# A decode step with cached attention, written anew on named semaphores: TensorE loops over the pairs, all queries come first, V stays a pair behind K

## The chip, the cores and the metric

The kernel runs on one core of a Trainium2 chip. The metric is the time of one execution on the device in microseconds; a kernel's time is the median of its runs. The engines are called as in the profile: PE (TensorE), DVE (VectorE), ACT (ScalarE), POOL (GpSimd) and SP (SyncE, which here issues DMAs); "SPq" is an issue by SP, "PEld" a weight load of PE.

## What is computed

One decode step for two tokens (one per batch entry), all in float32. `x` is normalised, attends with 32 heads to a cache of 8192 keys and values per head, and the result is gated by a small MLP:

```python
xn = layernorm(x)                                  # x: 2 x 1 x 512
q  = (xn @ wq), cut into 32 heads of 128           # wq: 512 x 4096
p  = softmax(q . k_cache * 128**-0.5)              # k_cache: 2 x 32 x 8192 x 128
s  = (p @ v_cache), heads side by side, @ wo       # wo: 4096 x 512
y  = layernorm(xn)
g  = silu(gelu(y @ w1 + b1) @ w2 + b2)             # w1: 512 x 1376, w2: 1376 x 512
out = x + s * g
```

K and V are 268 MB each; every byte is used once.

## The kernel before

The 64 (batch, head) rows are handled as 32 pairs, `n` = 0 to 31, of two heads each. A pair's K is one tile of 128 partitions x 128 rows x 128 columns, 8.39 MB: partitions 0 to 63 hold the first head, 64 to 127 the second, each partition 128 keys. A V tile looks the same. Three such tiles fill nearly all of the on-chip memory: two buffers for K (`kpool`) and one for V (`vpool`). At the start the second K buffer holds `wq` and the V buffer holds the start-up data: `w1`, `w2`, `x`, the normalised `x`, the projected queries, `sel`, `z` and `th` (`take`, L80 to 95).

The setup loads `w1`, `w2` and K0 (in two halves) from SP and the small inputs and `wq` from ACT. It normalises `x`, computes the MLP and its gate (`mlp`, L190 to 225; DVE writes `gate` at L224 and L225), projects the queries (`project_q`, L237), gathers them (`gather_q`, L247) and spreads the first pair's query over 128 partitions (`queries`, L258). Then SP issues K1 and V0 (L271, L272).

The loop over the pairs (L355 to 400) is written out by hand; each engine runs its instructions in the order of the program, and waits are put in by the framework from what reads and writes what. For pair `n`:

- DVE multiplies K by the query in two halves (L280) and sums over the columns in two halves (L285), which gives 128 scores per partition. The maximum over the free axis (L289) is transposed by PE (L293); DVE reduces it to one negative maximum per head (`nm`, L298) one half of a product *later*, in pair `n+1`.
- PE spreads `nm` over the partitions (L306), ACT copies it (L308) and takes the exponentials into `PZ` (L313). A matmul adds the row sums to `OA` (L319).
- PE multiplies V by the exponentials (`weighted`, L328: 32 calls, each two matmul instructions in the trace), ACT copies the result (L335), PE adds up the columns (L338), DVE spreads them (L343) and PE places them in `OA` (L351). The weighted sum for pair `n-1` stands in pair `n`.
- SP issues V of pair `n` when the weighted sum of `n-1` has released the one V buffer (L372), and K of `n+2` when DVE has summed pair `n` (L396).

Towards the end this order changes (`LATE`, L354): the weighted sums of the last pairs come a pair later, V30 goes into a K buffer, V31 is loaded in five pieces, and `wo` into the other K buffer in six (`WO_PIECES`, with the last two rows cut by partitions at 120, L404 to 407). At the end DVE divides `OA` by the row sums (L419, L421), PE multiplies by `wo` (`acc`, L424), DVE applies the gate and adds `x` (L428, L429), and SP and ACT store the two rows.

Of the kernel before, what the change touches and what calls it, by code (L numbers as in the profile page):

```python
# [1 line left out]

# [16 lines left out]
@with_exitstack  # L19
def decode_kernel(ctx: ExitStack, tc: tile.TileContext, x, kc, vc, wq, wo, w1, b1, w2, b2, out):  # L20
    nc = tc.nc
# [21 lines left out]
    ZP = P - U * PH  # L43

    consts = ctx.enter_context(tc.tile_pool(name="consts", bufs=1))
    kpool = ctx.enter_context(tc.tile_pool(name="kpool", bufs=2))
    vpool = ctx.enter_context(tc.tile_pool(name="vpool", bufs=1))
    small = ctx.enter_context(tc.tile_pool(name="small", bufs=2))
    ps_c = ctx.enter_context(tc.tile_pool(name="ps_c", bufs=1, space=bass.MemoryType.PSUM))
    ps_s = ctx.enter_context(tc.tile_pool(name="ps_s", bufs=4, space=bass.MemoryType.PSUM))  # L50
    ctx.enter_context(tc.manual_schedule())


    K, V = {}, {}
# [3 lines left out]
    def load(dst, src, cuts):  # L58
        for a, e in zip(cuts, cuts[1:]):
            nc.sync.dma_start(dst[:, a:e], src[:, a:e])  # L60

    def load_k(n, cuts=(0, KP)):
        K[n] = kpool.tile([P, KP, DH], F32, tag="k", name=f"k{n}")
        load(K[n], kf[n], cuts)

    def load_v(n, cuts=(0, KP), pool=vpool, tag="v"):
        V[n] = pool.tile([P, KP, DH], F32, tag=tag, name=f"v{n}")
        load(V[n], vf[n], cuts)


    PIECES = (0, 32, 64, 96, 112, 128)
    WO_PIECES = (0, 8, 16, 24, 30, 32)
# [12 lines left out]

    w1_sb = take(P, ND * F).rearrange("p (c f) -> p c f", f=F)
    w2_sb = take(P, (NF + 1) * D).rearrange("p (c n) -> p c n", n=D)
    x_sb = take(B, D)
    xn = take(B, D)
    y = take(B, D)  # L90
    b2_sb = take(1, D)
    q_nat = take(P, NG // QT * 512).rearrange("p (n c) -> p n c", c=512)
    sel = take(P, P)
    z = take(P, P)
    th = take(P, P)

    nc.scalar.dma_start(x_sb, x.rearrange("b s d -> (b s) d"))  # L97

    nc.sync.dma_start(w1_sb, w1.rearrange("(p c) f -> p c f", p=P))
    nc.sync.dma_start(w2_sb[:, :NF, :], w2[:NF * P, :].rearrange("(p c) n -> p c n", p=P))  # L100
    nc.sync.dma_start(w2_sb[:FT, NF, :], w2[NF * P:, :])
    load_k(0, (0, KP // 2, KP))


    b1_sb = consts.tile([P, NF + 1], F32, name="b1_sb")
    nc.vector.memset(b1_sb, 0.0)
    nc.scalar.dma_start(b1_sb[:, :NF], b1[:NF * P].rearrange("(p c) -> p c", p=P))
    nc.scalar.dma_start(b1_sb[:FT, NF:NF + 1], b1[NF * P:, None])
    nc.scalar.dma_start(b2_sb, b2[None, :])  # L109
    nc.scalar.dma_start(wq_sb, wq.rearrange("(p c) n -> p c n", p=P))  # L110


    ident = consts.tile([P, P], F32, name="ident")
    make_identity(nc, ident)
    ones = consts.tile([P, B], F32, name="ones")
    nc.vector.memset(ones, 1.0)
    srow = consts.tile([1, HP], F32, name="srow")
    nc.vector.memset(srow, SCALE)
    eps_t = consts.tile([B, 1], F32, name="eps_t")
    nc.vector.memset(eps_t, EPS)  # L120

    mod = consts.tile([P, R], F32, name="mod")

    blk = consts.tile([P, QT], F32, name="blk")

    half = consts.tile([P, U * PH], F32, name="half")
    nc.vector.memset(half, 0.0)
    for s in range(U):
        nc.vector.memset(half[HP * s:HP * (s + 1), PH * s:PH * (s + 1)], 1.0)

    Z = consts.tile([P, 2 * P - U * PH], F32, name="Z")
    ZR = consts.tile([P, 2 * P - U * PH], F32, name="ZR")
    nc.gpsimd.memset(Z, 0.0)
    nc.gpsimd.memset(ZR, 0.0)

    PZ = [consts.tile([P, NT, U, JW], F32, name=f"pz{n}") for n in range(3)]
    for t in PZ:
        nc.gpsimd.memset(t, 0.0)

    PO = [ps_c.tile([P, JW * DH], F32, name=f"po{n}") for n in range(2)]  # L140
    acc = ps_c.tile([P, P], F32, name="acc")
    OA = ps_c.tile([P, B, OC + 1], F32, name="OA")
    for t in PO + [acc]:
        nc.vector.memset(t, 0.0)

    zeros = PZ[2].rearrange("p t s j -> p (t s j)")
    nc.tensor.matmul(OA.rearrange("p b c -> p (b c)"), zeros[:, :P], zeros[:, :B * (OC + 1)],
                     start=True, stop=False)


    def layernorm(dst, src, name):
        st = small.tile([B, nc.vector.BN_STATS_DIM], F32, tag="st", name=f"st_{name}")
        nc.vector.bn_stats(st, src)
        mv = small.tile([B, nc.vector.BN_AGGR_DIM], F32, tag="mv", name=f"mv_{name}")
        nc.vector.bn_aggr(mv, st)
        sd = small.tile([B, 2], F32, tag="sd", name=f"sd_{name}")
        nc.scalar.activation(sd[:, 0:1], mv[:, 1:2], AF.Sqrt, bias=eps_t, scale=1.0)
        nc.vector.reciprocal(sd[:, 1:2], sd[:, 0:1])
        nc.vector.tensor_scalar(dst, src, mv[:, 0:1], sd[:, 1:2], op0=ALU.subtract, op1=ALU.mult)

    def transposed(src, name):

        p = ps_s.tile([P, P], F32, tag="s", name=f"pt_{name}")
        t = consts.tile([P, ND, B], F32, name=f"{name}T")
        for c in range(ND):
            nc.tensor.transpose(p[:, c * B:(c + 1) * B], src[:, c::ND], ident[:B, :B])
        nc.scalar.copy(t, p[:, :ND * B].rearrange("p (c b) -> p c b", b=B))  # L167
        return t


    x4 = consts.tile([P, P], F32, name="x4")
# [4 lines left out]
    nc.scalar.copy(x4, px)

    layernorm(xn, x_sb, "xn")
    by_row = ident.rearrange("p (j r) -> p r j", r=R)
    nc.vector.tensor_reduce(out=mod, in_=by_row, axis=AX.X, op=ALU.add)  # L180
    nc.vector.tensor_reduce(out=blk, in_=ident.rearrange("p (j r) -> p j r", r=R), axis=AX.X, op=ALU.add)
    layernorm(y, xn, "y")
    xnT = transposed(xn, "xn")
    yT = transposed(y, "y")


    gate = consts.tile([P, P], F32, name="gate")
    hT = consts.tile([P, NF + 1, B], F32, name="hT")

    def mlp():  # L190

        ph = ps_s.tile([P, P], F32, tag="s", name="ph")
        nc.vector.memset(ph[:, :(NF + 1) * B], 0.0)
        for f in range(NF + 1):
            for c in range(ND):
                w = w1_sb[:, c, f:NF * P:NF] if f < NF else w1_sb[:, c, NF * P:]
                nc.tensor.matmul(ph[:w.shape[1], f * B:(f + 1) * B], w, yT[:, c, :],  # L197
                                 start=(c == 0), stop=(c == ND - 1))

        shape = [P, NF + 1, B]  # L200
        h = small.tile(shape, F32, tag="gh", name="gh", bufs=1)
        p = ph[:, :(NF + 1) * B].rearrange("p (f b) -> p f b", b=B)
        nc.vector.tensor_tensor(out=h, in0=p, in1=b1_sb.unsqueeze(2).to_broadcast(shape), op=ALU.add)  # L203
        u = small.tile(shape, F32, tag="gu", name="gu", bufs=1)
        nc.vector.tensor_mul(u, h, h)
        nc.vector.tensor_scalar(u, u, GELU_A, 1.0, op0=ALU.mult, op1=ALU.add)
        nc.vector.tensor_mul(u, u, h)
        nc.scalar.activation(u, u, AF.Tanh, scale=GELU_C)
        nc.vector.scalar_tensor_tensor(u, u, 1.0, h, op0=ALU.add, op1=ALU.mult)
        nc.vector.tensor_scalar_mul(hT, u, 0.5)  # L210
        p = ps_s.tile([P, P], F32, tag="s", name="pgate")
        nc.vector.memset(p, 0.0)
        for f in range(NF + 1):
            m = P if f < NF else FT
            for j in range(QT):
                nc.tensor.matmul(p[R * j:R * j + B, :], hT[:m, f, :], w2_sb[:m, f, j * P:(j + 1) * P],
                                 start=(f == 0), stop=False)
# [8 lines left out]

    mlp()

    nc.gpsimd.memset(q_nat, 0.0)
    nc.vector.memset(sel, 0.0)
# [227 lines left out]
```

## Time and profile before

| | |
|---|---|
| time, median of 3 runs | 1312.75 us (1312.33 to 1313.4) |
| profiled execution: span from first to last instruction | 1308.4 us |
| what lies around the span, by the median | 4.35 us |
| mean granted TensorE clock | 0.628 |
| HBM read | 559.30 MB, 427 GB/s over the span |
| ACT busy, POOL busy | 83.9 us, 2.8 us |

The profiled execution is one of its own; its time as a run isn't listed, so its span is set against the median of the runs. The page gives each engine's busy time, and the span in forty slices of 32.7 us whose digits are busy tenths. It follows the chain of work that ended last back from the last instruction. A group row reads: line, engine, operation, tile written <- tiles read, shapes, count | busy us, mean ns of one | idle time of the engine ahead of it, and what ended most of that. A timeline row reads: start, duration, engine, line, operation; in brackets the idle time ahead of it and its releaser. An issue row reads: line, engine, operation, count, KB of each, us from issue to landing.

### The profile page before, as it was taken

What the parts mean: (1) busy time and instruction counts of PE and PEld (TensorE: products, weight loads), DVE (VectorE), ACT (ScalarE), POOL (GpSimd) and SP (SyncE); (2) the same over time, 40 slices, a digit from 0 to 9 for tenths busy, and PEclk for the clock granted to TensorE, in tenths of its full rate; (3) what the DMA queues carried; (4) which work ended last, traced back from release to release, by engine and by line L of the source; (5) the groups of instructions that cost most, each with busy time, mean ns of one, the idle gap of its engine ahead of it and who ended that gap; (6) DMA issues with size and microseconds to landing.
All of it is one profiled execution on the core that took longest, in us unless ns stands there. A gap on an engine that the chain in (4) does not pass through costs nothing.

```text
span 1308.4 us, 7376 instructions
## 1 busy us (share of the span) xinstructions
PE 445.0 (34%) x3258; PEld 173.7 (13%) x3258; DVE 1128.7 (86%) x261; ACT 83.9 (6%) x276; POOL 2.8 (0%) x12
## 2 busy tenths in 40 slices
PE   6403333322333321333332333332233332132166
PEld 6101111111111100111110111101111110010023
DVE  1399999988889988888988888998888998889980
ACT  1100000000000000000000000000000000000010
POOL 0000000000000000000000000000000000000000
PEclk9756666556666655666655666655666665565578
DMA  9999999999999999999999999999999999999997
GB/s 409 432 421 437 431 438 426 439 429 437 429 435 433 431 433 433 433 435 431 435 429 437 428 439 429 437 431 433 431 433 435 429 439 427 439 411 423 441 413 302
DMA packets 11517, 559.76 MB, mean 428 GB/s; under 512 B 1523, under 2 KB 1531, under 8 KB 1758
## 3 DMA queue, kind: packets, MB, share of 16 engines
q1 hardware_dynamic: 11071, 550.90, 97.7%
q10 hardware_dynamic: 414, 8.40, 1.5%
q8 instruction: 25, 0.41, 0.1%
q14 instruction: 7, 0.05, 0.0%
HBM read 559.30 MB, written 0.00 MB: 427 GB/s over the span
## 4 chain that ended last, share of the span: by engine, by line
DVE 50%; DMA 48%; PE 1%; issue 0%; ACT 0%; ACTq 0%; SPq 0%; DVEq 0%
DMA k<-in_A_k_cache_dram 42%; DVE k L280 25%; DVE sc L285 25%; DMA wq_sb<-in_A_wq_dram 3%; DMA wo_sb<-in_A_wo_dram 2%; PE pq L242 1%; PE acc L424 0%; DVE nm L298 0%; ACT boot L245 0%; PE pqa L252 0%; SPq L60 0%; ACTq L97 0%; ACTq L109 0%; DVE Z L343 0%; DVE mx L289 0%
## 5 line engine op out<-in xcount | busy, mean ns | idle before, releaser
L280 DVE TENSOR_TENSOR k<-k,q 128x8192 f32<-128x8192 f32 x64 | 555.5, 8680 | 110.0 <-DMA k<-in_A_k_cache_dram 92.2
L285 DVE TENSOR_REDUCE sc<-k 128x64 f32<-128x8192 f32 x64 | 552.4, 8666 | 0.0
L328 PE MATMUL po<-v,pz 128*8 128x512 f32 x2048 | 293.9, 738 | 191.1 <-DMA v<-in_A_v_cache_dram 191.1
L306 PE MATMUL pn<-nm,srow 1*64 1x1 f32 x128 | 11.7, 246 | 330.5 <-DVE nm L298 330.5
L328 PEld LDWEIGHTS po<-v,pz 128*8 128x8 f32 x2048 | 56.8, 103 | 410.3 <-issue 208.0
L293 PE MATMUL pm<-ident,mx 128*1 128x128 f32 x32 | 11.8, 368 | 234.6 <-DVE Z L343 176.6
L306 PEld LDWEIGHTS pn<-nm,srow 1*64 1x64 f32 x128 | 9.0, 193 | 334.6 <-DVE nm L298 334.5
L335 ACT COPY o<-po 128x512 f32<-128x512 f32 x32 | 18.8, 586 | 504.3 <-PE po L328 504.3
L308 ACT COPY bias<-pn 128x1 f32<-128x1 f32 x32 | 5.1, 160 | 589.2 <-PE pn L306 589.2
L338 PE MATMUL pt<-mod,o 128*128 128x2 f32 x256 | 33.7, 254 | 22.9 <-ACT o L335 22.9
L338 PEld LDWEIGHTS pt<-mod,o 128*128 128x128 f32 x256 | 31.0, 191 | 52.6 <-ACT o L335 52.6
L319 PE MATMUL OA<-ones,ZR 128*128 128x1 f32 x64 | 18.6, 359 | 51.8 <-ACT ZR L316 51.8
L293 PEld LDWEIGHTS pm<-ident,mx 128*1 128x1 f32 x32 | 2.5, 79 | 236.8 <-issue 201.6
L313 ACT ACTIVATE pz<-sc,bias 64x128 f32<-64x128 f32 x64 | 25.5, 399 | 1.4
L319 PEld LDWEIGHTS OA<-ones,ZR 128*128 128x128 f32 x64 | 15.8, 308 | 54.5 <-ACT ZR L316 54.5
L263 PE MATMUL pb<-q_all,ident 64*64 64x128 f32 x128 | 21.3, 433 | 0.3 <-ACT q_all L254 0.3
L343 DVE TENSOR_TENSOR Z<-blk,pt 128x8 f32<-128x8 f32 x32 | 4.9, 152 | 18.1 <-PE pt L338 18.1
L197 PE MATMUL ph<-yT,boot 128*128 128x2 f32 (+1 forms) x88 | 19.5, 359 | 0.3 <-ACT yT L167 0.3
L197 PEld LDWEIGHTS ph<-yT,boot 128*128 128x128 f32 (+1 forms) x88 | 19.4, 317 | 0.3 <-ACT yT L167 0.3
L203 DVE TENSOR_TENSOR gh<-ph,b_sb 128x22 f32<-128x22 f32 x1 | 0.2, 181 | 20.4 <-PE ph L197 20.4
L351 PE MATMUL OA<-mod,Z 128*128 128x32 f32 x64 | 15.3, 332 | 4.7 <-DVE Z L343 4.6
L351 PEld LDWEIGHTS OA<-mod,Z 128*128 128x128 f32 x64 | 15.8, 306 | 5.1 <-DVE Z L343 5.1
(81 smaller groups left out, 122.9 us busy)
## 6 DMA issues: line engine op xcount, KB each, us to landing
k<-in_A_k_cache_dram SPq DMA_DIRECT2D x2, 4096.0 KB, 46.2
v<-in_A_v_cache_dram SPq DMA_DIRECT2D x3, 2048.0 KB, 19.3
wo_sb<-in_A_wo_dram SPq DMA_DIRECT2D x3, 2048.0 KB, 22.0
boot<-in_B_w_dram SPq DMA_DIRECT2D x1, 2752.0 KB, 9.6
boot<-in_B_w_dram SPq DMA_DIRECT2D x1, 2560.0 KB, 15.5
v<-in_A_v_cache_dram SPq DMA_DIRECT2D x2, 1024.0 KB
wo_sb<-in_A_wo_dram SPq DMA_DIRECT2D x1, 1536.0 KB
k<-in_A_k_cache_dram SPq DMA_DIRECT2D x31, 42.7
```

The lines of the kernel that those rows point to most:

```text
L197: nc.tensor.matmul(ph[:w.shape[1], f * B:(f + 1) * B], w, yT[:, c, :], start=(c == 0), stop=(c == ND - 1))
L263: nc.tensor.matmul(p[HP * s:HP * (s + 1), :], w, q_all, start=True, stop=True)
L280: nc.vector.tensor_tensor(out=k, in0=k, in1=qb, op=ALU.mult)
L285: nc.vector.tensor_reduce(out=SC[n][:, a:e], in_=K[n][:, a:e, :], axis=AX.X, op=ALU.add)
L293: nc.tensor.transpose(p[:1, :], MX[n], ident)
L306: nc.tensor.matmul(p[HP * s:HP * (s + 1), :1], srow, nm[:, s:s + 1], start=True, stop=True)
L313: nc.scalar.activation(PZ[n % 3][r, :, s, :], sc[r], AF.Exp, bias=bias[r], scale=SCALE, accum_out=rs[r])
L319: nc.tensor.matmul(OA[:, b, OC:], ZR[:, a:a + P], ones[:, :1], start=False, stop=False)
L328: nc.tensor.matmul(po[R * j:R * j + U * JW, :], pz[:, t].rearrange("p s j -> p (s j)"), v[:, t * JW:(t + 1) * JW, :].rearrange("p j d -> p ...
L335: nc.scalar.copy(o4, PO[n % 2])
L338: nc.tensor.matmul(PT[n][:, :U], o4[:, i * DH:(i + 1) * DH], mod[:, i:U * JW:JW], start=(i == 0), stop=(i == JW - 1))
L351: nc.tensor.matmul(OA[:, b, :OC], Z[:, a:a + P], mod, start=False, stop=(n == N - 1))
```

## The change

The kernel is written anew without the framework's pools and automatic waits. A small class issues each instruction with the semaphores it waits for and the one that it counts up:

```python
    def take(self, eng, name, v=1):
        self.engines[eng].wait_ge(self.sem(name), v).then_inc(self.sem(name), -v)

    def op(self, eng, method, *args, waits=(), sig=None, quiet=False, **kwargs):
        need = self.need(eng, waits)
        for name, v in need[:-1]:
            self.engines[eng].wait_ge(self.sem(name), v)
        ins = getattr(self.engines[eng], method)(*args, **kwargs)
        for name, v in need[-1:]:
            ins._wait_ge(self.sem(name), v)
...
        ins.then_inc(self.sem(name), by)
```

Each engine still runs its instructions in the order in which they are written. What differs:

- **Loads at the start.** All but `x` come from SP, in the order `w1`, `w2`, `b1`, `b2`, `wq`, K0 in one piece.
- **Queries ahead.** `Q` holds the queries of all 32 pairs. PE computes them in eight groups of four pairs, ACT copies each group, and DVE clears `po` behind the seventh copy, ahead of pair 0.
- **The gate.** PE computes the MLP's second product behind the queries. DVE's instruction for `gate` stands behind pair 0's `nm`. SP waits for it ahead of V0, which overwrites `th` and `z`.
- **The pairs.** DVE takes a pair in one product and one sum of 128x16384, then the maximum, then waits for PE's transpose and reduces it to `nm` before it goes to the next pair. `PZ`, `po` and `o4` have one buffer each. PE runs a loop of 31 rounds (`Fori`) of `weighted` and `softmax`; its semaphores are counted down as they are taken.
- **Loads in the loop.** K of `n+2` and V of `n+1`, to the end. V31 goes into the first K buffer in one piece, and `wo` into the V buffer in pieces of 24, 5, 2 and 1 rows.
- **Placing once.** The columns of each pair are kept in `OT`, the row sums in `RS`; after the last pair DVE spreads both at once (`Z`, `ZL`) and PE places them with four calls.

The diff, cut to its core:

```diff
-    load_k(0, (0, KP // 2, KP))
-    nc.scalar.dma_start(wq_sb, wq.rearrange("(p c) n -> p c n", p=P))
+    op("SP", "dma_start", b1_sb[:, :NF], b1[:NF * P].rearrange("(p c) -> p c", p=P), sig="d_b")
+    op("SP", "dma_start", b1_sb[:, NF:], b1[F - P:, None], sig="d_b")
+    t["b"] = op("SP", "dma_start", b2_sb, b2[None, :], sig="d_b")
+    op("SP", "dma_start", wq_sb, wq.rearrange("(p c) n -> p c n", p=P), sig="d_wq")
+    k_land = {0: op("SP", "dma_start", KBUF[0], kf[0], sig="d_k0")}
...
+    for g in range(N // NPB):
+        t[f"Q{g}"] = op("ACT", "copy", Q[:, g * NPB:(g + 1) * NPB, :],
+                        PB[g % 2].rearrange("p (n d) -> p n d", d=DH), waits=[pe(f"pb{g}")])
...
+    t["po0"] = op("DVE", "memset", po, 0.0, waits=[t[f"Q{N // NPB - 2}"]])
+    t["acc0"] = op("DVE", "memset", acc, 0.0, waits=[t["qall"]])
+    t["z"] = op("ACT", "copy", z, pgate, waits=[pe("pgate")])
+    t["th"] = op("ACT", "activation", th, z, AF.Tanh, scale=0.5, waits=[t["z"]])
+    op_k1 = op("SP", "dma_start", KBUF[1], kf[1], sig="d_k1", waits=[pe("pq"), ("d_wq", 16)])
...
-    for n in range(NG // QT):
-        project_q(n)
-    gather_q()
-    queries(0)
-    load_k(1)
-    load_v(0)
...
-    for n in range(N):
-        scores_mul(n, 0, M)
-        if n:
-            max_dve(n - 1)
-            if n < LATE:
-                exps(n - 1)
-        scores_mul(n, M, KP)
-        if n + 1 < N:
-            queries(n + 1)
...
+    for n in range(N):
+        k = KBUF[n % U]
+        if n:
+            op("ACT", "copy", o4, po, sig="s_o4", waits=[pe_n("p_v", n - 1)])
+            t["OT"] = op("ACT", "copy", OT[:, U * (n - 1):U * n], pt[:, :U], waits=[pe_n("p_t", n - 1)])
+        qb = Q[:, n, :].unsqueeze(1).to_broadcast([P, KP, DH])
+        a = op("DVE", "tensor_tensor", out=k, in0=k, in1=qb, op=ALU.mult, waits=[k_land[n], Qt[n]])
+        a = op("DVE", "tensor_reduce", out=SC[n % 2], in_=k, axis=AX.X, op=ALU.add, waits=[a], sig="v_k")
+        k_done = a
+        op("DVE", "tensor_reduce", out=MX, in_=SC[n % 2], axis=AX.X, op=ALU.max, waits=[a], sig="v_mx")
+        op("DVE", "tensor_reduce", out=nm, in_=pm[:1, :P].rearrange("o (s r) -> o s r", s=U), axis=AX.X,
+           op=ALU.max, negate=True, waits=[pe_n("p_m", n)], sig="v_nm")
+        if n == 0:
+            a = op("DVE", "scalar_tensor_tensor", gate, th, 1.0, z, op0=ALU.add, op1=ALU.mult,
+                   waits=[t["th"], t["pool"]])
+            t["gate"] = a
+            wait("SP", t["gate"], t["sel"], t["qnat"], pe("pgate"))
+            op("SP", "dma_start", VB, vf[0], sig="d_v")
...
+        m = n + 2
+        if m < N:
+            k_land[m] = op("SP", "dma_start", KBUF[m % U], kf[m], sig=f"d_k{m % U}", waits=[k_done])
+            op("SP", "dma_start", VB, vf[m - 1], sig="d_v", waits=[pe_n("p_v", m - 2)])
+        elif m == N:
+            op("SP", "dma_start", KBUF[m % U], vf[N - 1], sig="d_v31", waits=[k_done])
+            wait("SP", pe_n("p_v", N - 2))
+            wo_v = wo.rearrange("(p c) n -> p c n", p=P)
+            for i, (c0, c1) in enumerate(zip(WO_CUTS, WO_CUTS[1:])):
+                op("SP", "dma_start", wo_sb[:, c0:c1], wo_v[:, c0:c1], sig=f"d_wo{i}")
...
+    for g in range(N // NPB):
+        queries(g)
+    for f in range(NF + 1):
+        for j in range(QT):
+            mm(pgate[R * j:R * j + B, :], hT[:, f, :], w2_sb[:, f, j * P:(j + 1) * P], start=f == 0, stop=False,
+               waits=[t["hT"], t["w2"], t["mem"]])
...
+    def softmax():
+        take("PE", "v_mx")
+        op("PE", "transpose", pm[:1, :P], MX, ident, sig="p_m")
+        take("PE", "v_nm")
+        for s in range(U):
+            mm(pn[HP * s:HP * (s + 1), :1], srow, nm[:, s:s + 1], sig="p_n" if s == U - 1 else None)
+
+    def weighted(v, last=False):
+        take("PE", "s_pz", U)
...
+            take("PE", "d_v", 16)
+        for i in range(NT):
+            j = i % QT
+            mm(po[R * j:R * j + U * JW, :], PZ[:, i].rearrange("p s j -> p (s j)"),
+               v[:, i * JW:(i + 1) * JW, :].rearrange("p j d -> p (j d)"), start=i < QT, stop=i + QT >= NT,
+               sig="p_v" if i == NT - 1 else None)
+        take("PE", "s_o4")
...
+    softmax()
+    with nc.tensor.Fori(0, N - 1):
+        weighted(VB)
+        softmax()
+    weighted(KBUF[0], last=True)
```

More of the change, by code (lines that the diff above doesn't have):

```diff
@@ L113, in decode_kernel @@
[L113 to L127, printed above, removed]
@@ L128, in decode_kernel @@
-    for s in range(U):
[L129 to L159, printed above, removed]
@@ L176, in decode_kernel @@
[L176 to L217, printed above, removed]
-        for j in range(QT):
-            nc.tensor.matmul(p[R * j:R * j + B, :], ones[:1, :B], b2_sb[:, j * P:(j + 1) * P],
-                             start=False, stop=True)
-        nc.scalar.copy(z, p)
-        nc.scalar.activation(th, z, AF.Tanh, scale=0.5)
-        nc.vector.scalar_tensor_tensor(th, th, 1.0, z, op0=ALU.add, op1=ALU.mult)
-        nc.vector.tensor_scalar_mul(gate, th, 0.5)
@@ new lines, in decode_kernel @@
+    x_sb = boot(B, D)
+    xn = boot(B, D)
+    y = boot(B, D)
+    b2_sb = boot(1, D)
+    q_nat = boot(P, NG // QT * 512).rearrange("p (n c) -> p n c", c=512)
+    sel = boot(P, P)
+    z = boot(P, P)
+    th = boot(P, P)
+    q_all = boot(BH, DH)
+    wq_sb = big[1].rearrange("p (c n) -> p c n", n=H * DH)
+    wo_sb = big[2].rearrange("p (c n) -> p c n", n=D)
+    Q = sb([P, N, DH], "Q")
+    ident = sb([P, P], "ident")
+    ones = sb([P, B], "ones")
+    srow = sb([1, HP], "srow")
+    eps_t = sb([B, 1], "eps_t")
@@ new lines, in decode_kernel @@
+    mod = sb([P, R], "mod")
+    blk = sb([P, QT], "blk")
+    half = sb([P, U * PH], "half")
+    b1_sb = sb([P, NF + 1], "b1_sb")
+    x4 = sb([P, P], "x4")
+    gate = sb([P, P], "gate")
+    res = sb([P, P], "res")
+    xnT = sb([P, ND, B], "xnT")
+    yT = sb([P, ND, B], "yT")
+    hT = sb([P, NF + 1, B], "hT")
+    gh = sb([P, NF + 1, B], "gh")
+    gu = sb([P, NF + 1, B], "gu")
+    SC = [sb([P, KP], f"sc{i}") for i in range(2)]
+    MX = sb([P, 1], "MX")
+    nm = sb([1, U], "nm")
+    bias = sb([P, 1], "bias")
@@ new lines, in decode_kernel @@
+    op("POOL", "memset", PZ, 0.0)
+    t["pool"] = op("POOL", "memset", gate, 0.0)
+    op("DVE", "memset", eps_t, EPS)
+    op("DVE", "memset", ones, 1.0)
+    op("DVE", "memset", srow, SCALE)
+    a = op("DVE", "memset", half, 0.0)
+    for s in range(U):
+        t["half"] = op("DVE", "memset", half[HP * s:HP * (s + 1), PH * s:PH * (s + 1)], 1.0, waits=[a])
+    a = op("DVE", "memset", sel, 0.0)
+    for k in (1, 2, 6):
+        t["mem"] = op("DVE", "memset", bank[k], 0.0)
+    by_row = ident.rearrange("p (j r) -> p r j", r=R)
@@ new lines, in decode_kernel @@
+    a = op("DVE", "reciprocal", rl, OA[:, :, OC], waits=[pe_n("p_oa", 0)])
+    t["on"] = op("DVE", "tensor_tensor", out=on, in0=OA[:, :, :OC], in1=rl.unsqueeze(2).to_broadcast([P, B, OC]),
+                 op=ALU.mult, waits=[a])
+    a = op("DVE", "scalar_tensor_tensor", res, acc, 0.5, gate, op0=ALU.mult, op1=ALU.mult,
+           waits=[pe_n("p_acc", 0), t["gate"], t["acc0"]])
+    t["res"] = op("DVE", "tensor_add", res, res, x4, waits=[a, t["x4"]])
+    for b, eng in enumerate(("SP", "ACT")):
+        t[f"o{b}"] = op(eng, "dma_start", out[b, 0].rearrange("(j n) -> j n", n=P), res[b::R, :], sig=f"d_o{b}",
+                        waits=[t["res"]])
+        wait(eng, t[f"o{b}"])
@@ new lines, in decode_kernel, with mm, transposed @@
+    done = []
+    def mm(dst, w, v, start=True, stop=True, sig=None, waits=(), skip=False):
+        kw = {"skip_group_check": True} if skip else {}
+        if sig in PE_EVENTS:
+            done.append(sig)
+            sig = "pe_setup"
+        return op("PE", "matmul", dst, w, v, start=start, stop=stop, waits=waits, sig=sig, quiet=sig is None, **kw)
+    def transposed(dst, src, after, name):
+        for c in range(ND):
+            last = c == ND - 1
+            if last:
+                done.append(name)
+            op("PE", "transpose", dst[:, c * B:(c + 1) * B], src[:, c::ND], ident[:B, :B], waits=[after, t["ident"]],
+               sig="pe_setup" if last else None, quiet=not last)
@@ L239, in project_q @@
+    transposed(pxn, xn, t["xn"], "xnT")
+    transposed(py, y, t["y"], "yT")
+    for f in range(NF + 1):
+        for c in range(ND):
+            w = w1_sb[:, c, f:NF * P:NF] if f < NF else w1_sb[:, c, F - P:]
+            last = f == NF and c == ND - 1
+            mm(ph[:, f * B:(f + 1) * B], w, yT[:, c, :], start=c == 0, stop=c == ND - 1,
+               waits=[t["yT"], ("d_w1", 16)], sig="ph" if last else None)
+    for n in range(NG // QT):
         for c in range(ND):
@@ L421, in decode_kernel @@
-    nc.vector.tensor_tensor(out=on, in0=OA[:, :, :OC], in1=rl.unsqueeze(2).to_broadcast([P, B, OC]), op=ALU.mult)
-    for c in range(OC):
-        for j in range(QT):
-            nc.tensor.matmul(acc[R * j:R * j + B, :], on[:, :, c], wo_sb[:, c, j * P:(j + 1) * P],
-                             start=(c == 0), stop=(c == OC - 1))
-    r = small.tile([P, P], F32, tag="res", name="res", bufs=1)
-    nc.vector.tensor_mul(r, acc, gate)
-    nc.vector.tensor_add(r, r, x4)
-    for b in range(B):
-        eng = nc.sync if b % 2 == 0 else nc.scalar
-        eng.dma_start(out[b, 0].rearrange("(j n) -> j n", n=P), r[b::R, :])
+                last = n == NG // QT - 1 and c == ND - 1 and j == QT - 1
@@ new lines, in decode_kernel @@
+                mm(PQ[n][R * j:R * j + B, :], xnT[:, c, :], wq_sb[:, c, g * 512:(g + 1) * 512], start=c == 0,
+                   stop=c == ND - 1, waits=[t["xnT"], t["mem"], ("d_wq", 16)], sig="pq" if last else None)
+    for n in range(NG // QT):
+        for hh in range(HG):
+            a = HP - (n * QT * HG + hh)
+            last = n == NG // QT - 1 and hh == HG - 1
+            mm(pqa[:BH, :], sel[:, a:a + BH], q_nat[:, n, hh * DH:(hh + 1) * DH], start=n + hh == 0, stop=last,
+               waits=[t["sel"], t["qnat"]], sig="pqa" if last else None)
@@ new lines, in queries @@
+    def queries(g):
+        for i in range(NPB):
+            n = g * NPB + i
+            for s in range(U):
+                w = ident[:BH, U * n + s:U * n + s + 1].to_broadcast([BH, HP])
+                last = i == NPB - 1 and s == U - 1
+                mm(PB[g % 2][HP * s:HP * (s + 1), i * DH:(i + 1) * DH], w, q_all,
+                   waits=[t["qall"]] + ([t[f"Q{g - 2}"]] if g > 1 else []) + ([t["hT"]] if g == 1 else []),
+                   sig=f"pb{g}" if last else None)
+    for g in range(N // NPB):
+        queries(g)
@@ new lines, in decode_kernel @@
+    wait("PE", t["po0"], t["pool"], t["mod"])
+    softmax()
[3 more added lines that the diff above has]
+    weighted(KBUF[0], last=True)
+    for b in range(B):
+        h = slice(b * H, (b + 1) * H)
+        mm(OA[:, b, :OC], Z[:, h].rearrange("p h r -> p (h r)"), mod, waits=[t["Z"]])
+        m = slice(b * HH, (b + 1) * HH)
+        mm(OA[:, b, OC:], ZL[:, m].rearrange("p n r -> p (n r)"), ones[:, :1], sig="p_oa" if b == B - 1 else None)
+    for i, (c0, c1) in enumerate(zip(WO_CUTS, WO_CUTS[1:])):
+        for c in range(c0, c1):
+            for j in range(QT):
+                last = c == OC - 1 and j == QT - 1
+                mm(acc[R * j:R * j + B, :], on[:, :, c], wo_sb[:, c, j * P:(j + 1) * P], start=c == 0,
+                   stop=c == OC - 1, waits=[t["on"], t["acc0"], (f"d_wo{i}", 16)], sig="p_acc" if last else None)
```

348 lines of the change are left out of this document (146 added, 202 removed).

## The prediction

> **What bounds the kernel now.** I read the page from the top (busy shares, the forty slices, the queues), then the chain of work that ended last.
>
> ```profile
> span 1308.4 us, 7376 instructions
> ...
> PE 445.0 (34%) x3258; PEld 173.7 (13%) x3258; DVE 1128.7 (86%) x261; ACT 83.9 (6%) x276; POOL 2.8 (0%) x12
> ...
> DMA  9999999999999999999999999999999999999997
> ...
> DMA packets 11517, 559.76 MB, mean 428 GB/s; under 512 B 1523, under 2 KB 1531, under 8 KB 1758
> ...
> q8 instruction: 25, 0.41, 0.1%
> ...
> k<-in_A_k_cache_dram SPq DMA_DIRECT2D x31, 42.7
> v<-in_A_v_cache_dram SPq DMA_DIRECT2D x31, 29.4
> ```
>
> DVE is busy 86% of the span, but the DMA row is full from the first slice to the last but one. Every byte of K and V is read once, so a stretch without transfers is never made good. The chain shows the floor of the stream:
>
> ```profile
> 194.99 36.94 DMA k<-in_A_k_cache_dram
> ...
> 266.72 42.83 DMA k<-in_A_k_cache_dram
> ...
> 344.34 42.61 DMA k<-in_A_k_cache_dram
> ...
> 421.74 43.37 DMA k<-in_A_k_cache_dram
> ...
> 1121.03 42.84 DMA k<-in_A_k_cache_dram
> ```
>
> Columns: start, duration. These K tiles land at 231.93, 309.55, 386.95, 465.11 and 1163.87, two pairs (four tiles of 8.39 MB) apart. The shortest step is 77.40 us, 19.35 per tile or 38.70 per pair; the steps of 77.62 and 78.16 are above it. From 231.93 to 1163.87 are twelve steps: 931.94 us, 3.1 above twelve floors. So: a floor that does not move, plus a small excess.
>
> A pair costs DVE less than that:
>
> ```profile
> L280 DVE TENSOR_TENSOR k<-k,q 128x8192 f32<-128x8192 f32 x64 | 555.5, 8680 | 110.0 <-DMA k<-in_A_k_cache_dram 92.2
> ...
> 249.51 17.20 DVE sc L285 x2
> ...
> 90.16 0.29 DVE L289 TENSOR_REDUCE mx<-sc 128x1 f32<-128x128 f32 x1
> ...
> 90.50 0.37 PE L293 MATMUL pm<-ident,mx 128*1 128x128 f32 x1 [34.99 <-DVE mx L289]
> ...
> 98.97 0.27 DVE L298 TENSOR_REDUCE nm<-pm 1x2 f32<-1x128 f32 x1
> ```
>
> Two halves of sums take 17.20, two of products as much: 34.4 us, and DVE has waited 92.2 us for K in all. DVE has slack; the stream has none. The two rows of K and V issues on the page say the same: 42.7 and 29.4 us from issue to landing are 23 and 10 us more than a tile's 19.35, so a load is always issued while others are still ahead of it.
>
> **The change, part by part.** The bytes stay the same, and so does the steady order of loads (K of pair n+2, V of n+1, K of n+3). I go through the places where the stream could run dry.
>
> *Setup.* The rows of before:
>
> ```profile
> 0.74 0.54 ACTq L97 DMA_DIRECT2D boot<-in_A_x_dram  x1
> ...
> 2.67 0.68 DVE L153 BATCH_NORM_STATS2 st_xn<-boot 2x6 f32<-2x512 f32 x1
> ...
> 37.03 0.29 DVE L224 SCALAR_TENSOR_TENSOR boot<-boot 128x128 f32<-128x128 f32 x1 [5.30 <-ACT boot L223]
> ...
> 42.53 8.43 PE L242 MATMUL pq<-wq_sb,xnT 128*2 128x512 f32 x64 [6.21 <-DMA wq_sb<-in_A_wq_dram]
> ...
> 53.43 1.09 PE L252 MATMUL pqa<-boot 128*64 128x128 f32 x8 [1.45 <-ACT boot L245]
> ...
> 54.55 0.26 ACT L254 COPY q_all<-pqa 64x128 f32<-64x128 f32 x1 [1.18 <-PE pqa L252]
> ...
> 54.66 0.33 SPq L60 DMA_DIRECT2D v<-in_A_v_cache_dram  x1
> ...
> 54.87 0.65 PE L263 MATMUL pb<-q_all,ident 64*64 64x128 f32 x8 [0.35 <-ACT q_all L254]
> ...
> 55.65 8.69 DVE L280 TENSOR_TENSOR k<-k,q 128x8192 f32<-128x8192 f32 x1 [17.72 <-ACT q L265]
> ...
> 111.69 0.33 SPq L60 DMA_DIRECT2D v<-in_A_v_cache_dram  x1
> ...
> v<-in_A_v_cache_dram SPq DMA_DIRECT2D x1, 23.3
> ```
>
> The last row is the issue at 111.69, the load of V1: 23.3 us later, at 135.0, it had landed. The loads ahead of it were K1, V0, K2, so at 19.35 each V0 landed at 96.3, K1 at 76.9 and K0 at 57.5, with no gap: V0 was issued at 54.66, long before K1 was through.
>
> In the new kernel V0 goes into the buffer that holds the start-up data (weights of the MLP, z, th), and SP waits for the token of `gate` before it issues V0. The gate's instruction stands on DVE *behind pair 0's product, sum, maximum and nm*; before, it ran at 37.03, ahead of them. So V0 cannot be issued until DVE has been through all of K0. Behind that wait on SP stand V0 (TensorE's first weighted sum waits for it) and K2 (DVE's pair 2), which waits for pair 0's sums anyway. K1 is no problem: it waits for the projections, done while K0 still lands. But between K1's landing and V0's issue nothing is queued, and the stream stops.
>
> When does pair 0 start? K0 has the same bytes ahead of it as before, now all in SP's queue: 57.5 or a little earlier. wq is ahead of K0, one tile earlier: 38.1 at the latest. Then follow 8.43 (projections), two copies of 128x512 at about 0.6 (o4's copy, below), 2 x 1.09 (gathering), 0.3 for q_all: 50.3. All the queries now come ahead of pair 0, 64 calls in eight groups, and DVE clears the accumulator `po` only when the seventh group has been copied, ahead of pair 0's product in its order. A pair's query is 4 instructions; the row shows 8 in 0.65 us, 0.081 each, so seven groups of 16 take 9.1: 59.5, with a copy and two memsets (0.6 + 0.7) 60.8. If wq lands two us earlier, as its bytes no longer share with K0, 59; if the instructions overlap better when many stand in a row, 56, and then K0 is the later one. I take 58.5. It moves nothing else: DVE waited until 55.65 before, too.
>
> Then 34.4 for product and sum: 92.9. From the start of the maximum to that of TensorE's transpose 0.34, its 0.37, a hop of 0.1, nm 0.27, gate 0.3: V0 is issued at about 94.3. From issue to first use an idle queue took 1.93 us for x (0.74 to 2.67), so V0 lands at 94.3 + 1.9 + 19.35 = 115.6 instead of 96.3. **The gap costs 19.3 us.**
>
> *The steady loop.* After the gap K2 lands a tile behind V0 at 135, DVE has long done pair 1, and the period is the stream's again if nothing else is longer. DVE: 34.4 + 0.3 + 0.5 + 0.3 = 35.5 us, as it now waits for TensorE's transpose, with the next pair's product queued behind it; margin 3.2 us to 38.70. TensorE:
>
> ```profile
> 102.42 9.20 PE L328 MATMUL po<-v,pz 128*8 128x512 f32 x64
> 111.70 0.59 ACT L335 COPY o<-po 128x512 f32<-128x512 f32 x1 [8.89 <-PE po L328]
> 112.34 1.05 PE L338 MATMUL pt<-mod,o 128*128 128x2 f32 x8 [0.72 <-ACT o L335]
> ```
>
> From V's landing it is 9.2 us until its buffer is free and the next V can be issued, 19.35 - 9.2 = 10 us before the stream would run dry; with copy and columns 11 us, so TensorE is free some 4 us before the next maximum comes. No gap and no gain: the fewer instructions of TensorE, the placements (Z, ZR and OA per pair) and the single buffers for PZ and po lie beside the transfers. If that cover were gone, every us over the period would cost 31.
>
> *The excess.* From V0 (96.3) to wo's last landing, 1301.2 (rows below), before took 1204.9; 62 tiles at 19.35 are 1199.7. Excess 5.2. The traffic that is neither inputs nor outputs is the code, the 25 packets of the q8 row. TensorE's loop makes most of that unnecessary, and all else is small. Bounds: the whole excess stays (0) or goes (-5.2). I take -4.
>
> *The end.*
>
> ```profile
> 1269.93 31.28 DMA wo_sb<-in_A_wo_dram
> ...
> 1276.22 9.39 PE L328 MATMUL po<-v,pz 128*8 128x512 f32 x64
> 1288.66 4.91 PE L424 MATMUL acc<-wo_sb,on 128*2 128x128 f32 x128 [0.52 <-DVE on L421]
> 1295.86 1.93 PE L424 MATMUL acc<-wo_sb,on 128*2 128x128 f32 x64 [2.30 <-DMA wo_sb<-in_A_wo_dram]
> 1301.25 3.45 PE L424 MATMUL acc<-wo_sb,on 128*2 128x128 f32 x64 [3.46 <-DMA wo_sb<-in_A_wo_dram]
> 1304.74 0.29 DVE L428 TENSOR_TENSOR res<-acc,gate 128x128 f32<-128x128 f32 x1 [16.14 <-PE acc L424]
> ```
>
> Before, wo lands at 1301.21 and the accumulation ends 3.5 later. Now wo is the last tile, 19.4 behind V31. From V31's landing: the weighted sum, 9.4; from its end (1285.6) to the first acc 3.1 before, for which I take 4.4, as Z and ZL are now computed and placed for all pairs at once: 13.8. The first 24 rows of wo land at 24/32 x 19.4 = 14.6. Their 192 instructions at 4.91/128 take 7.4, the other 64 between 1.93 and 3.45: 23.9 to 25.4, that is 4.5 to 6 us after the last landing; at 1.93/64 throughout, 2.9. The smaller last piece brings nothing, as TensorE is behind. I take 1.3 us more than before.
>
> **The sum** on the profiled execution: 1308.4 + 19.3 - 4 + 1.3 = 1325.0. The runs' median is 1312.75, 4.35 above that span; with this carried over, 1329.4. A measurement of this kernel tells about 0.2% (2.6 us) from no change.
>
> **Rivals.**
>
> *The loop's branch costs code transfers (0.13).* A pair's body on TensorE is 64 + 8 + 1 + 4 matmuls and as many weight loads. If each of 31 returns fetched a block like the 25 (0.41 MB / 25 = 16 KB), the excess would be 31/25 x 5.2 = 6.4 instead of 1.2, 1334.6. If they all fell on the same of the 16 engines, the price of one is at least 78.16 - 77.40 = 0.76, 31 of them 23.6, 1352. For it: the code has to come from somewhere. Against: 6516 matmuls and weight loads in 0.41 MB are 63 bytes each, so a body of some 160 is 10 KB, less than a block. A stall of TensorE itself would be hidden: the branch stands ahead of the wait for V.
>
> The Trainium skill, "Runtime: NRT & Kernel Launch", section "Instruction fetch mechanics", speaks against the change here: a taken branch to a target outside the two-page window forces a fetch before execution goes on. Whether this body crosses a page no run here shows; by that rule the time would be this rival's.
>
> *Slow queries (0.08).* In the loop a query takes twice as long:
>
> ```profile
> 1199.41 0.69 PE L263 MATMUL pb<-q_all,ident 64*64 64x128 f32 x4
> ```
>
> At 0.69/4 seven groups are 19.3 us, pair 0 starts at 70, V0 goes out 11.5 us later: 1341. Against it: TensorE comes from 8 us of projections here, and out of an idle stretch there.
>
> *The loop has a longer chain than I see (0.05).* Softmax of pair n on TensorE stands behind the weighted sum of n-1, so a late V delays nm, DVE and the next K. It begins when DVE's 35.5 plus the delay pass 38.70; each us beyond is 31 in the end: 1345 for half a us.
>
> *Not slower (0.04).* The gap is repaid because 38.70 is no floor but the pace at which SP got buffers. New order and earlier frees would have to bring 16.6/31 = 0.54 us per pair, a period of 38.3 against 38.83 now; from there it is no slower than 1312.75. Against it: K and V are issued with 23 and 10 us of queue left (above), so SP's frees don't set the pace. That V0 is issued early after all would do the same, from an issue at 78; DVE's order excludes it.
>
> **How the numbers follow.** Forecast 0.70: 1329.4. Inside it the start of pair 0 (56 to 61), the excess (0 to -5.2) and the end (-0.6 to +2.5) give 1324 to 1337. Range 1321 to 1342: it takes in the slow queries and the spread form of the branch rival, and leaves the single engine, the long chain and the repaid gap out. Faster 0.03, same 0.02, slower 0.95.
>
> **What would show it.** Right: among the forty slices one (32.7 us) with half the DMA time empty, within 75 to 97; V0 issued at 92 to 97, just behind the gate on DVE; K landings in the loop 77.4 apart; PE's acc ending 4 to 6 us behind wo. Fewer q8 packets say that the code stays; as many as 31 more say the branch fetches. Wrong: V0 issued ahead of 80, no empty slice, or a period other than 38.7.

## The result and the profile after

The changed kernel takes 1325.34 us in the median (four runs, 1324.34 to 1325.7), the kernel before 1313.04 in four runs, the three of the table above and one more (1312.33 to 1313.4): a ratio of 1.0098, 95% interval 1.0084 to 1.0113. The change costs about 12 us, 1%. The profiled executions' spans are 1308.4 and 1322.9 us, 14.5 apart; why this is more than the medians' 12.3 is taken up with the carry from span to time, below.

From the page of the changed kernel (busy time, the transfers in forty slices of 33.1 us, the code queue):

```profile
span 1322.9 us, 7003 instructions
...
PE 396.9 (30%) x3128; PEld 144.7 (11%) x3128; DVE 1129.2 (85%) x166; ACT 70.5 (5%) x244; POOL 1.1 (0%) x8
...
DMA  9939999999999999999999999999999999999997
GB/s 413 427 159 444 432 424 442 430 429 442 430 428 442 430 428 442 434 424 442 438 420 442 438 420 442 440 418 440 442 418 440 442 418 440 442 418 440 442 418 318
...
q8 instruction: 6, 0.10, 0.0%
```

DVE does the same work as before, PE less. One thing sticks out: in the third slice, 66 to 99 us, the DMA engines are busy three tenths of the time. No other slice but the last is below nine tenths. The timeline of the changed kernel says why (start, duration, engine, line, operation, idle time ahead and its releaser; all operations are recorded by one helper, so they all have line 51; PEq is TensorE's sequencer):

```profile
4.27 42.44 SPq L51 DMA_DIRECT2D big<-in_A_k_cache_dram  x2
...
57.52 17.21 DVE L51 TENSOR_TENSOR big<-big,Q 128x16384 f32<-128x16384 f32 x1
...
74.76 17.22 DVE L51 TENSOR_REDUCE sc<-big 128x128 f32<-128x16384 f32 x1
92.01 0.29 DVE L51 TENSOR_REDUCE MX<-sc 128x1 f32<-128x128 f32 x1
92.44 0.37 PE L51 MATMUL bank<-ident,MX 128*1 128x128 f32 x1 [31.05 <-PEq L45]
92.85 0.28 DVE L51 TENSOR_REDUCE nm<-bank 1x2 f32<-1x128 f32 x1 [0.56 <-PE bank L51]
93.06 0.27 DVE L51 SCALAR_TENSOR_TENSOR gate<-big 128x128 f32<-128x128 f32 x1
...
93.36 0.33 SPq L51 DMA_DIRECT2D big<-in_A_v_cache_dram  x1
...
93.74 0.42 SPq L51 DMA_DIRECT2D big<-in_A_k_cache_dram  x1
...
115.38 9.25 PE L51 MATMUL bank<-big,PZ 128*8 128x512 f32 x64 [21.72 <-PEq L45]
```

The first row is the issue of K0 at 4.27 and of K1 at 46.4. K1's issue row (us to landing) is:

```profile
big<-in_A_k_cache_dram SPq DMA_DIRECT2D x1, 29.6
```

So K1 lands at 76.0. After K1 SP issues nothing until 93.36, when gate on DVE has ended: V0, and K2 behind it. From 76.0 to 93.36 nothing is queued. TensorE gets V0 at 115.38; before, it had landed at 96.3.

Behind this the loop runs at the stream's pace, as two products on DVE near the end show:

```profile
1219.67 17.23 DVE L51 TENSOR_TENSOR big<-big,Q 128x16384 f32<-128x16384 f32 x1 [3.07 <-DMA big<-in_A_k_cache_dram]
...
1249.86 0.16 ACT L51 COPY OT<-bank 128x2 f32<-128x2 f32 x1 [1.21 <-PE bank L51]
1254.18 0.28 DVE L51 TENSOR_REDUCE MX<-sc 128x1 f32<-128x128 f32 x1
...
1258.38 17.23 DVE L51 TENSOR_TENSOR big<-big,Q 128x16384 f32<-128x16384 f32 x1 [3.08 <-DMA big<-in_A_k_cache_dram]
```

They start 38.71 apart, and DVE waits 3.1 us for K in each pair. The end, first from the timeline, then the issues of wo (KB, us to landing):

```profile
1287.89 1.75 SPq L51 DMA_DIRECT2D big<-in_A_wo_dram  x4
...
1297.09 8.90 PE L51 MATMUL bank<-big,PZ 128*8 128x512 f32 x64 [2.56 <-DMA big<-in_A_v_cache_dram]
...
1310.16 0.22 DVE L51 TENSOR_TENSOR on<-bank,rl 128x64 f32<-128x64 f32 x1
1311.66 8.54 PE L51 MATMUL bank<-big,on 128*2 128x128 f32 x256 [1.74 <-DMA big<-in_A_wo_dram]
...
1320.99 0.61 SPq L51 DMA_DIRECT2D out_dram<-res  x1
```

```profile
big<-in_A_wo_dram SPq DMA_DIRECT2D x1, 6144.0 KB, 23.7
...
big<-in_A_wo_dram SPq DMA_DIRECT2D x1, 256.0 KB, 27.3
```

The last of four issues starts at about 1289.2, so wo's last row lands at 1316.5. With that the 14.5 us divide into three parts:

| part of the span | before | after | difference |
|---|---|---|---|
| start to V0's landing | 96.3 | 115.3 | +19.0 |
| V0's landing to wo's last | 1204.9 | 1201.2 | -3.7 |
| wo's last landing to the end of the span | 7.2 | 6.4 | -0.8 |

### The profile page after: what moved, and what is told of

It is laid out like the page before. It is cut to its first block, busy times and chain, and to the rows that moved or that the text cites. A ratio compares the mean times of both kernels' runs of the same rounds, so it can differ in the third digit from the quotient of the medians.

```text
span 1322.9 us, 7003 instructions
## 1 busy us (share of the span) xinstructions
PE 396.9 (30%) x3128; PEld 144.7 (11%) x3128; DVE 1129.2 (85%) x166; ACT 70.5 (5%) x244; POOL 1.1 (0%) x8
## 5 line engine op out<-in xcount | busy, mean ns | idle before, releaser
L51 DVE TENSOR_TENSOR big<-big,Q 128x16384 f32<-128x16384 f32 x32 | 551.2, 17224 | 96.1 <-DMA big<-in_A_k_cache_dram 96.1
L51 DVE TENSOR_REDUCE sc<-big 128x128 f32<-128x16384 f32 x32 | 551.0, 17220 | 1.1
L51 PE MATMUL bank<-big,PZ 128*8 128x512 f32 x2048 | 287.9, 725 | 689.2 <-PEq L45 686.7
L51 PEld LDWEIGHTS bank<-big,PZ 128*8 128x8 f32 x2048 | 59.7, 102 | 890.4 <-issue 887.8
L51 ACT COPY o<-bank 128x512 f32<-128x512 f32 x32 | 18.7, 585 | 939.8 <-PE bank L51 939.8
L51 PE MATMUL bank<-mod,o 128*128 128x2 f32 x256 | 32.8, 250 | 25.7 <-PEq L45 25.7
L51 PEld LDWEIGHTS bank<-mod,o 128*128 128x128 f32 x256 | 31.0, 191 | 54.4 <-issue 54.4
L51 ACT ACTIVATE PZ<-sc,bias 64x128 f32<-64x128 f32 x64 | 25.5, 399 | 1.9
L51 DVE TENSOR_REDUCE nm<-bank 1x2 f32<-1x128 f32 x32 | 8.9, 279 | 17.8 <-PE bank L51 17.8
L51 PE MATMUL bank<-yT,big 128*128 128x2 f32 x88 | 19.9, 364 | 1.9 <-DMA big<-in_B_w_dram 1.9
L51 PEld LDWEIGHTS bank<-yT,big 128*128 128x128 f32 x88 | 19.9, 322 | 2.0 <-DMA big<-in_B_w_dram 2.0
```

Of the source, the lines that this page charges most:

```text
L51: ins = getattr(self.engines[eng], method)(*args, **kwargs)
```

## The experiments

The kernel before ran beside the experiments too. Its median was 1311.53 us beside the first four and 1310.59 beside the fifth, against 1313.04 beside the changed kernel. So a difference of medians between an experiment and the changed kernel is good to some 1.5 us; for anything smaller the traces have to speak.

**1. Tiles of their own for z and th.** SP then needn't wait for gate ahead of V0, only for the MLP's second product.

```diff
-    z = boot(P, P)
-    th = boot(P, P)
+    z = sb([P, P], "z")
+    th = sb([P, P], "th")
...
-            wait("SP", t["gate"], t["sel"], t["qnat"], pe("pgate"))
+            wait("SP", t["sel"], t["qnat"], pe("pgate"))
```

> The changed kernel, with tiles of their own for z and th, so that SP's wait ahead of V0 is for the MLP's second product (which ends at 61.4) and no longer for gate. My theory (the stream stands still from K1's landing at 76.0 until V0 is issued at 93.4, and nothing gives that back): V0 is issued at about 61.5, lands one tile behind K1 at 95.3 instead of 115.2, everything behind it moves by as much, span 1303 and time 1305.5, faster than both kernels. Rival A (the steady loop is what costs, DVE's wait for TensorE in each pair or the counted-down semaphores, and the gap is beside it): stays within 3 us of 1325. Rival B (the excess over the floor went because the gap let all queues start level, not because there is less code): V0 to wo's last landing goes from 1201.3 back to about 1205, time 1309.

Measured: 1306.11 us (1304.3 to 1307.51), 0.9962 of the kernel before (0.995 to 0.9974); span 1304.4. The timeline of this kernel:

```profile
59.80 0.33 SPq L51 DMA_DIRECT2D big<-in_A_v_cache_dram  x1
...
91.80 0.33 SPq L51 DMA_DIRECT2D big<-in_A_k_cache_dram  x1
...
95.73 8.42 PE L51 MATMUL bank<-big,PZ 128*8 128x512 f32 x64 [2.28 <-PEq L45]
...
1277.25 9.86 PE L51 MATMUL bank<-big,PZ 128*8 128x512 f32 x64 [2.57 <-DMA big<-in_A_v_cache_dram]
```

V0 is issued 33.6 us earlier, but arrives 19.65 earlier (95.73 for 115.38): it now stands behind K1 in the queue instead of behind an idle one. The span is 18.5 shorter, the median 19.2. So the whole of the loss, and more, sits in this one wait; rival A falls. The time is near the expected 1305.5. From V0's use to V31's are 1181.5 us, in the changed kernel 1181.7 (1297.09 - 115.38): the excess did not come back with the unbroken stream, and rival B falls as far as V31. Behind it one late step remains, in the issues of wo:

```profile
big<-in_A_wo_dram SPq DMA_DIRECT2D x1, 256.0 KB, 29.6
```

The last row comes 2.3 us later behind its issue than the 27.3 of the changed kernel; the three pieces ahead of it are 0.7 to 0.8 later. The trace shows what stood ahead of its last packets. The transfers that start between 1296 and 1296.25, and between 1296.25 and 1297:

```profile
q8 instruction: 1, 0.02, 26.6%
...
DMA packets 0, 0.00 MB, mean 0 GB/s; under 512 B 0, under 2 KB 0, under 8 KB 0
```

A packet of code begins, and its 26.6% of 16 engines in 0.25 us are 1.06 us of one engine. No other packet starts until it is through; wo's last three follow from 1297.15 on. That is about one of the 2.3 us; what made the rest is not shown. TensorE was still working on the rows ahead of them.

**2. The loop written out.**

```diff
-    with nc.tensor.Fori(0, N - 1):
+    for _ in range(N - 1):
         weighted(VB)
         softmax()
```

> The changed kernel with TensorE's loop written out 31 times; nothing else is different. Theory (code transfers made the excess): the q8 packets go from 6 back to about 25, V0 to wo's last landing from 1201.3 to about 1205, the time from 1325.3 to 1329. Rival B (the gap had levelled the queues): the landings stay 77.40 apart, 1325.3. Rival C (the branch itself costs something on the path): 1 to 3 us faster. If the part of the time that lies outside the span (2.4 us in the changed kernel, 4.4 before) depends on how much code there is, it grows here too.

Measured: 1328.56 us (1328.48 to 1328.9), 1.0132 of before (1.0118 to 1.0147); span 1327.6. The changed kernel's range ends at 1325.7. From its page and its timeline:

```profile
q8 instruction: 25, 0.41, 0.1%
```

```profile
115.50 8.78 PE L51 MATMUL bank<-big,PZ 128*8 128x512 f32 x64 [21.64 <-PEq L45]
...
1300.43 8.53 PE L51 MATMUL bank<-big,PZ 128*8 128x512 f32 x64 [2.89 <-DMA big<-in_A_v_cache_dram]
```

The gap is unchanged, V0 is used at 115.50; from there to V31 it is 1184.9 instead of 1181.7. Nineteen more blocks of code on q8 come with 3.2 us on the stream and 3.2 us on the median. The starts of DVE's products show where these 3.2 us are:

```profile
562.02 17.22 DVE L51 TENSOR_TENSOR big<-big,Q 128x16384 f32<-128x16384 f32 x1 [3.06 <-DMA big<-in_A_k_cache_dram]
...
600.90 17.22 DVE L51 TENSOR_TENSOR big<-big,Q 128x16384 f32<-128x16384 f32 x1 [3.24 <-DMA big<-in_A_k_cache_dram]
...
640.54 17.23 DVE L51 TENSOR_TENSOR big<-big,Q 128x16384 f32<-128x16384 f32 x1 [4.01 <-DMA big<-in_A_k_cache_dram]
...
679.25 17.23 DVE L51 TENSOR_TENSOR big<-big,Q 128x16384 f32<-128x16384 f32 x1 [3.07 <-DMA big<-in_A_k_cache_dram]
```

The first two of these steps, 38.88 and 39.64, have one q8 packet each, the third, 38.71, has none. So it is from 134.75 to the last product at 1261.38: the 11 steps without a q8 packet take 38.69 to 38.71 us, and the whole excess over 38.70, 4.3 us, lies in eight of the 18 steps with one. In the changed kernel the excess is 1.4 us there, nearly all of it in two steps (39.33 and 39.43), and these have code packets too: two on q14, the other queue of code, and one on q8. So it is the code that made most of the excess over the floor; neither the levelling by the gap nor the branch explains it. What decides which packet costs time is not shown: ten of the 18 steps with one take 38.72 at most.

The time outside the span is 1.3 us here and 1.4 in the changed kernel, so it doesn't follow the amount of code. (The 2.4 and 4.4 of the expectation set a profiled span against the median of other runs.)

**3. The wait made longer.** One more sum on DVE ahead of gate, over K1, which has landed by then; its result is overwritten unused.

```diff
-        a = op("DVE", "tensor_tensor", out=k, in0=k, in1=qb, op=ALU.mult, waits=[k_land[n], Qt[n]])
+        a = op("DVE", "tensor_tensor", out=k, in0=k, in1=qb, op=ALU.mult, waits=[k_land[n], Qt[n], t.get("hold")])
...
         if n == 0:
+            t["hold"] = op("DVE", "tensor_reduce", out=SC[1], in_=KBUF[1], axis=AX.X, op=ALU.add, waits=[k_land[1]])
             a = op("DVE", "scalar_tensor_tensor", gate, th, 1.0, z, op0=ALU.add, op1=ALU.mult,
```

> The changed kernel with one more sum over K1 (17.2 us, its result is overwritten unused) on DVE ahead of gate: the suspected wait is made 17.2 longer. Theory: V0 is issued at 110.6 instead of 93.4 and the time grows by the same 17.2, to 1342.5, one for one. If later stages have slack that absorbs some of the gap, less than that; if DVE were the bound in the loop, its lost 17.2 would cost the same, but then the landings behind would not stay 77.4 apart.

Measured: 1342.17 us (1341.06 to 1342.78), 1.0235 of before (1.022 to 1.025). From its timeline:

```profile
93.71 17.20 DVE L51 TENSOR_REDUCE sc<-big 128x128 f32<-128x16384 f32 x1
110.84 0.27 DVE L51 SCALAR_TENSOR_TENSOR gate<-big 128x128 f32<-128x128 f32 x1
...
111.14 0.33 SPq L51 DMA_DIRECT2D big<-in_A_v_cache_dram  x1
...
133.25 7.25 PE L51 MATMUL bank<-big,PZ 128*8 128x512 f32 x44 [38.94 <-PEq L45]
...
1314.69 5.74 PE L51 MATMUL bank<-big,PZ 128*8 128x512 f32 x32 [2.58 <-DMA big<-in_A_v_cache_dram]
```

V0 is issued 17.8 us later than in the changed kernel (17.2 of them the added sum); the span is 17.9 longer (1340.8), the median 16.8 higher. From V0's use to V31's are 1181.4 us, as without it: nothing behind the gap gives any of it back. (In the last two rows some of the 64 records are missing; only their starts are used.)

**4. wo in two pieces.**

```diff
-    WO_CUTS = (0, 24, 29, 31, 32)
+    WO_CUTS = (0, 24, 32)
```

> The changed kernel with wo in two pieces of 24 and 8 rows instead of 24, 5, 2 and 1. Prediction's claim: the small last pieces bring nothing, because TensorE starts on the 24 rows at 1311.7 and still works on them when the last row lands at 1316.6: 1325.3 within 0.4. Rival: TensorE catches up and waits for the eight rows, 1 to 3 us slower.

Measured: 1326.32 us (1325.36 to 1327.43), 1.0116 of before (1.0101 to 1.0131). That is 1.0 above the changed kernel's median, with ranges that overlap, and outside the 0.4 of the expectation. Half of it lies around the span: 1.9 us in each of its runs, 1.3 to 1.4 in the changed kernel's, and no run here shows why. The spans' medians are 1324.45 and 1324.0. V0's issue in its setup, and the chain at the end:

```profile
94.40 0.33 SPq L51 DMA_DIRECT2D big<-in_A_v_cache_dram  x1
```

```profile
1312.76 0.09 issue
1312.85 8.91 PE bank L51 x256
```

In this execution V0 is issued 1.04 later than in the changed kernel's profiled one, in a setup that is the same code, and TensorE starts on wo 1.19 later (1312.85 for 1311.66). The 256 matmuls on wo run in one piece of 8.91 us: TensorE did not stop for the eight rows. By their issue they land at about 1317.7 (29.6 us behind it), and TensorE comes to them after three quarters of its work, at about 1319.5. The claim about the pieces holds by the trace; by the times alone this run doesn't decide it.

**5. Pieces at the end, on top of the first experiment.**

```diff
+    V_CUTS = (0, 64, 96, 112, 128)
-    WO_CUTS = (0, 24, 29, 31, 32)
+    WO_CUTS = (0, 8, 16, 24, 28, 30, 31, 32)
...
-            op("SP", "dma_start", KBUF[m % U], vf[N - 1], sig="d_v31", waits=[k_done])
+            for i, (a0, a1) in enumerate(zip(V_CUTS, V_CUTS[1:])):
+                op("SP", "dma_start", KBUF[m % U][:, a0:a1], vf[N - 1][:, a0:a1], sig=f"d_v31_{i}", waits=[k_done])
...
+            if last and i * JW in V_CUTS:
+                nc.tensor.wait_ge(pr.sem(f"d_v31_{V_CUTS.index(i * JW)}"), 16)
```

> The first experiment's kernel (tiles of their own for z and th), with V31 in four pieces of 64, 32, 16 and 16 rows and wo in seven of 8, 8, 8, 4, 2, 1 and 1, TensorE waiting for each. In the first experiment TensorE begins V31's weighted sum when all of it has landed (1277.2), has the divided outputs at 1292.3, and then works 9.2 us on wo, to 1301.6, though wo's last row landed at 1298.3 and would have at 1296.7 without one late step. Theory (with the stream unbroken, only what stands behind the last landing is left): the outputs are ready some 6 us behind V31 (1283), wo is taken as it lands, the accumulation ends 0.5 to 1 us behind the last landing instead of 3.4 to 5: span 1300 to 1302, time 1301.5 to 1303.5, 2.5 to 4.5 faster than the first experiment. Rival (smaller pieces slow the stream, as more DMAs and shorter rows are issued): wo's last landing moves back by 1 us or more, and the time stays at 1305 or above.

Measured: 1303.5 us (1302.42 to 1304.72), 0.9943 of before (0.993 to 0.9957): the fastest kernel here, 2.6 below the first experiment's median. Its timeline:

```profile
1272.34 0.29 DVE L51 TENSOR_REDUCE MX<-sc 128x1 f32<-128x128 f32 x1
...
1275.03 0.18 ACT L51 ACTIVATION_READ_ACCUMULATOR PZ<-sc,bias 64x1 f32 x1
1275.36 9.53 PE L51 MATMUL bank<-big,PZ 128*8 128x512 f32 x64 [1.38 <-PEq L45]
...
1290.24 9.16 PE L51 MATMUL bank<-big,on 128*2 128x128 f32 x256 [0.61 <-DVE on L51]
```

The time is at the upper edge of the expected range, but not for the expected reason. V31's weighted sum starts not with the first piece but at 1275.36, right behind the exponentials, which wait for DVE to finish pair 31. That is 1.9 us earlier than in the first experiment (1277.25). Of these 0.7 are there already when pair 31's product starts (1237.82 for 1238.52), so the pieces of V31 account for some 1.2. The outputs are divided at 1290.1, not at 1283, and TensorE still needs 9.2 us for wo. So the small pieces of wo bring nothing that the trace shows; what was gained is V31's earlier start. The rival falls: wo's last row lands at about 1296.9 (the last of seven issues starts at about 1268.8, and the last two take 28.1 us), for 1298.3 in the first experiment.

## Why the prediction was right, step by step

- **Where the time goes: right.** V0 was issued at 93.36 (forecast 94.3) and used at 115.38 (115.6); the gap is worth 19.0 (19.3). Experiments 1 and 3 show the cause: with the wait gone the span is 18.5 us shorter and the median 19.2, with 17.2 added the span is 17.9 longer and the median 16.8.
- **When pair 0 starts: 57.52 for 58.5.** The queries set it, not K0, which landed at 56.5 (52.2 us behind its issue): the two memsets ahead of the first product wait for ACT's copy, as forecast. The queries ran faster than the row of before on which I had leaned, 128 instructions in 7.29 us, 0.057 each for 0.081; the slow form of the rivals fell:

```profile
49.76 7.29 PE L51 MATMUL bank<-big,ident 64*64 64x128 f32 x128 [0.35 <-ACT big L51]
...
56.98 0.63 DVE L51 MEMSET bank<- 128x512 f32 x2 [25.07 <-ACT Q L51]
```

- **The loop: right.** DVE waits 3.1 us per pair (margin forecast 3.2), and TensorE is through with the columns by 1249.86, 4.3 ahead of the next maximum at 1254.18 (forecast 4). The rival of a longer chain fell.
- **The excess: right**, -3.7 for -4 (from one execution of each), and for the reason given, as experiment 2 shows. That the size came so near is in part luck: the forecast took 4 between bounds of 0 and 5.2, and in experiment 2 one code packet cost anything from nothing to 1.2 us. The branch rival fell: six packets on q8, with 31 returns. On the Trainium skill's rule ("Runtime: NRT & Kernel Launch", "Instruction fetch mechanics") a fetch is due when a branch leaves the window; the six packets say that this body of some 160 instructions did not.
- **The end: mis-sized**, -0.8 for +1.3. The outputs were ready 13.3 behind V31 (forecast 13.8), and TensorE began on wo 14.6 behind V31, when its first 24 rows had landed, as summed. But the 256 matmuls on wo took 8.54 us where I had summed 9.3 to 10.9; in experiments 1 to 5 they took 8.83 to 9.84, so this execution is a quick one. They ended 3.7 behind wo's last landing, just short of the 4 to 6 that I had named as a sign. And between the issue of the last store and the end of the span lie 1.9 us now (1320.99 to 1322.9); before there were 3.0, which the forecast had carried over unseen:

```profile
1305.39 0.62 SPq L432 DMA_DIRECT2D out_dram<-res  x1
```

- **The carry from span to time: wrong**, and 3.0 of the miss of 4.1 us; the spans of the changed kernel's four runs have a median of 1324.0, against 1325.0 in the sum. I had set the profiled span of before against the median of other runs and taken the 4.35 us between them as what lies around a span. The changed kernel's profiled execution had 1324.34 with a span of 1322.9, 1.4 us around it; its other runs had 1.3 to 1.4. Later timed executions of before had about 1.8 (1313.11 with a span of 1311.3, 1309.65 with 1307.9). The profiled execution of before has no time on record; if 1.8 lay around its span too, it took 1310.2, one of the quicker ones of a kernel whose runs reach from 1308.95 to 1313.46 over all comparisons. By this, 2.5 of the 4.35 were the spread of before. It is also most of the reason why the profiled spans differ by 14.5 and the medians by 12.3. What makes this spread no run here settles.
- **Not slower** needed the gap to be repaid at 0.54 us per pair. It was not: experiment 3 finds the same 1181.4 us behind a gap that is 17.8 longer.

## What to carry to other kernels

In a kernel whose DMA engines are always busy, look for the one stretch in which nothing is queued: follow each load back to the last instruction whose token its buffer waits for, and to what stands ahead of that instruction on its engine. Here a 0.27 us instruction behind 35 us of other work cost 19 us, and two small tiles of their own gave them back. A part's worth is read from the queue, not from the wait: V0's issue moved by 33.6 us and the time by 19.2, as beyond K1's landing there was nothing more to gain.

## What was not expected of the hardware

- Code transfers delay a full stream: 19 blocks of 16 KB more, 0.31 MB of 560, cost 3.2 us, while their bytes at the mean rate of 422 GB/s would take 0.7. The one block looked at closely (experiment 1) held one DMA engine for 1.06 us.
- TensorE's loop of 31 rounds caused no code transfers that can be seen: 6 packets with the loop, 25 without. Only one of the 6 falls between pair 2 and pair 31.
- The setup of one and the same code moves by about a us between executions (V0's issue at 93.36 and at 94.40), and in the changed kernel such a us goes through to the end, as V0's issue sets the rest (experiment 3: V0 17.8 later, the span 17.9 longer).
